# A feed-forward stage: a subtraction on another engine, a sum replaced by a read, and a block's products moved to the group's end

## Chip, cores and metric

The kernel runs on one core of a Trainium2 chip. The metric is the device time of one execution in microseconds, as the median of several runs. A core has TensorE (PE in the profile, with PEld for its weight loads), VectorE (DVE), ScalarE (ACT), GpSimd (POOL) and SyncE (SP). SP, ACT and POOL can each issue DMAs.

## The reference, cut to what matters

```python
# attention with a decay bias, 4 batches x 8 heads x 576 tokens x 64  ->  x [2304, 512]
h = x @ w_in                                   # w_in [512, 2048]
g = where(h >= 1, h, where(h <= -1, 0, (h + 1) ** 2 / 4))
x2 = g @ w_out                                 # w_out [2048, 512]
logits = x2 @ w_gate                           # [2304, 8]
# 8 experts with 288 tokens each, taken greedily by logit;
# out[mask] = relu(x2[mask] @ w1[e]) @ w2[e]
```

Each operand of the feed-forward products is split into a high part (`xh`, `ih`, `gh`, `oh`: a copy rounded to the matmul's float type) and a low part (`xl`, `il`, `gl`, `ol`: operand minus high part), and a product is the sum of three matmuls, high by high, high by low and low by high. The weights arrive as 64-bit numbers; the kernel converts them to 32-bit ones during the attention and keeps these in device memory, in the buffers `w32` (the flag `wide`).

## The kernel before, in words

Attention comes first, then the feed-forward, then routing and the experts. The change lies in the feed-forward (class `Ffn`).

The 2304 tokens go through in six groups of 384, numbered 0 to 5 here; each group goes through the 16 blocks of 128 columns of the hidden layer. The text calls a block's work `h(i)` (12 matmuls into the PSUM tile `ph`, of which there are three, L619) and `xmm(i)` (nine matmuls that add the block's part of x2 to the three PSUM tiles `px`, L656 to L658). Programs are written out in full, so every engine runs its own instructions in the order in which `run` issues them.

Between `h(i)` and `xmm(i)` stands a chain over three engines: VectorE clips `ph` to [-1, 1] (L627, "the clip"), ScalarE squares (L628), VectorE takes the maximum with `ph` (L639, "the maximum"), ScalarE copies the result into `gh` (L640), and GpSimd subtracts, `gl = u - gh` (L641). The finished pair waits in the list `pend` until two blocks are there; then the older one's `xmm` is issued. So `xmm(i)` comes after `h(i+2)` on TensorE, and blocks 14 and 15 of a group are added up after `h(0)` and `h(1)` of the next group. Then `tail` copies the three `px` tiles out (L665) and stores them.

At the end of each group but the last, the next group's x is split: right behind `h(15)` four ScalarE copies make `xh` (L605) and four VectorE subtractions `xl` (L606), since `h(15)` is the last to read the old ones.

VectorE also has a list of small jobs, `later`, taken up a few at a time: one by `some(1)` between the clip and the maximum, and three by `some(3)` at the block's end, from block 3 of group 1 on. These are the "dots": for each of the 8 experts a 128 x 512 multiplication with a gate row, summed along the row (L677). 120 of them make the logits of x2's rows (input `x`). 128 of them fold the gate into w_out (input `wt`, one 128 x 512 tile of w_out for 8 dots; two buffers). `fold` makes that tile on GpSimd as `oh + ol` (L706), each one issued with the first dot of the tile before it. The last group keeps its pairs (tiles `ghk`, `glk`), gets its logits by matmuls with the folded weights, and its products follow in `rest`.

In group 0 further work is on VectorE and GpSimd: the last steps of the attention (`norm`, `side_last`, called by `first(i)`) and the splits of the weights (`split_hi`, `split_lo`, L583 and L591).

Of the kernel before, what the change touches and what calls it, by code (L numbers as in the profile page):

```python
# [9 lines left out]
F32 = mybir.dt.float32  # L10
# [8 lines left out]
OP = mybir.AluOpType  # L19
# [5 lines left out]
def f(t):  # L25
    return t.bitcast(F32)
# [7 lines left out]
class Attention:  # L34
# [23 lines left out]
    def setup(self, identf):  # L58
        nc, c = self.nc, self.c
        S = self.S  # L60
        self.identf = identf
        st = self.w.tile([32, S], F32, name="s_in", tag="El")
        nc.scalar.dma_start(st, self.s.rearrange("b h s -> (b h) s"))
        self.load_first(0)
        zero = c.tile([128, 128], F32, name="zero")
# [63 lines left out]
        for h in range(2):  # L129
            nc.sync.dma_start(f(W)[64:66, h, :S], f(ck)[h:h + 1])  # L130
# [13 lines left out]
    def first_pair(self, h):  # L144

        X, Y, Z, W = self.stacks[0]
        for which in (1, 0):
            self.copy_hi(0, which, (h,))
        self.nc.gpsimd.tensor_scalar(Z[0:64, h], f(X)[0:64, h], 1.0, 0.0, op0=OP.mult, op1=OP.add)
        self.nc.vector.tensor_copy(Y[64:128, h, :self.S], f(Y)[0:64, h, :self.S])  # L150
        for which in range(2):
            self.prep_lo(0, which, (h,))
# [305 lines left out]
class Ffn:  # L458
# [3 lines left out]

    G = 384

    def __init__(self, tc, dr, raw, xp, t, xd, w_in, w_out, w_gate, x2d, L, wog, identf):
# [127 lines left out]
    def xload(self, g):  # L595
        self.xg = self.t.tile([128, 4, self.G], F32, name="xg", bufs=1)
        self.nc.sync.dma_start(self.xg, self.xd[:, g * self.G:(g + 1) * self.G].rearrange("(c p) t -> p c t", p=128))

    def xsplit(self):
        nc, G = self.nc, self.G  # L600
        self.x = []
        for c in range(4):
            xh = self.t.tile([128, G], F32R, name=f"xh{c}", bufs=1)
            xl = self.t.tile([128, G], F32R, name=f"xl{c}", bufs=1)
            nc.scalar.activation(xh, self.xg[:, c], AF.Copy)  # L605
            nc.vector.tensor_tensor(xl, self.xg[:, c], f(xh), op=OP.subtract)  # L606
            self.x.append((xh, xl))

    def h(self, i, keep, prep, x, x0):

        nc, G = self.nc, self.G
        ih, il = self.W["i", i]
        p = self.ps.tile([128, 512], F32, name="ph", tag="ph", bufs=3)
        n = 0
        for c in range(4):
            xh, xl = self.x[c]
            s = slice(c * 128, c * 128 + 128)
            for a, b in ((ih, xh), (ih, xl), (il, xh)):
                nc.tensor.matmul(p[:, :G], a[:, s], b, start=n == 0, stop=n == 11)  # L619
                n += 1  # L620
        if x:
            self.xsplit()
        if prep and i:
            self.split_hi("i", i + 2)

        u = self.t.tile([128, G], F32, name="u")
        nc.vector.tensor_scalar(u, p[:, :G], -1.0, 1.0, op0=OP.max, op1=OP.min)  # L627
        nc.scalar.activation(u, u, AF.Square, bias=self.half, scale=0.5)  # L628
        if prep and i:
            self.split_lo("i", i + 2)  # L630
        if not x0:
            self.some(1)
        if keep:
            gh = self.w[i // 8].tile([128, G], F32R, name="ghk", tag=f"ih{i}")
            gl = self.w[i // 8].tile([128, G], F32R, name="glk", tag=f"il{i}")
        else:
            gh = self.t.tile([128, G], F32R, name="gh", bufs=3)
            gl = self.t.tile([128, G], F32R, name="gl", bufs=3)
        nc.vector.tensor_tensor(u, p[:, :G], u, op=OP.max)  # L639
        nc.scalar.activation(gh, u, AF.Copy)  # L640
        (nc.vector if keep and i == self.NF - 1 else nc.gpsimd).tensor_tensor(gl, u, f(gh), op=OP.subtract)  # L641
        if prep:
            self.split_hi("o", i + 1)
            self.split_lo("o", i + 1)
            for j in {3: (), 4: ()}.get(i, (8, 9, 10) if i == 5 else (i + 5,)):
                self.load_in(j)
                self.load_out(j)
        return gh, gl
# [50 lines left out]

    def fold(self, i):  # L700

        oh, ol = self.W["o", i]

        def add():
            self.wt[i] = self.gp.tile([128, 512], F32, name="wt", bufs=2)
            self.nc.gpsimd.tensor_tensor(self.wt[i], f(oh), f(ol), op=OP.add)  # L706

        return add, self.dots(lambda: self.wt[i], self.wogf[:, i])

    def fold_split(self):  # L710
        nc, w, wf = self.nc, self.wog, self.wogf
# [56 lines left out]
    def run(self, ntok, first, second):  # L768

        nc, NF = self.nc, self.NF  # L770
        NG = ntok // self.G
        pend, later, ready = [], self.later, None
        for g in range(NG):
            end = g == NG - 1
            if end:
                self.fold_split()
            px, pl, own = [], None, []
            if not g:

                px += [self.ps.tile([128, 512], F32, name="px", tag="px", bufs=4) for _ in range(3)]  # L780
            for i in range(NF):
                if i == 2 and not end:
                    self.xload(g + 1)
                gp = self.h(i, end, g == 0, i == NF - 1 and not end, g == 1 and i < 3)
                if i == 2 and not end and g:
                    px += [self.ps.tile([128, 512], F32, name="px", tag="px", bufs=4) for _ in range(3)]
                if not g and i == 2:

                    p = self.ps.tile([128, 512], F32, name="busy", tag="px", bufs=4)
                    for _ in range(6):  # L790
                        nc.tensor.matmul(p[:, :self.G], self.W["i", 2][0][:, :128], self.x[0][0], start=True,
                                         stop=True)
                if len(pend) == 2 or (end and pend):
                    j, a, b, p, gg = pend.pop(0)
                    self.xmm(j, a, b, p, range(3))
                    if j == NF - 1:
                        ready = (gg, p)
                if end:
                    own.append(gp)
                    if i == 0:  # L800
                        pl = self.ps.tile([128, 512], F32, name="pl", tag="px", bufs=4)
                    if i >= 2:
                        self.logits(i - 2, *own[i - 2], pl)
                else:
                    pend.append((i,) + gp + (px, g))
                if ready:
                    gg, p = ready
                    ready = None
                    tails = [(3 * gg + t, self.tail(3 * gg + t, p[t])) for t in range(3)]
                    dots = [d for tt, x2 in tails for d in self.dots(lambda x2=x2: x2, self.L[:, tt])]  # L810
                    later[:0] = dots
                if g == 0:
                    first(i)
                if g > 1 - (i > 2) and (not end or i % 2 or i < 8):
                    self.some(1 if end else 3)
                if g == 0 and i == NF - 2:
                    second()
            if g == 0:

                adds, dots = zip(*[self.fold(i) for i in range(NF)])  # L820
                adds[0]()
                for i in range(NF):
                    nxt = adds[i + 1] if i + 1 < NF else lambda: None
                    later += [lambda a=nxt, d=dots[i][0]: (a(), d())] + dots[i][1:]
        self.some(len(later))
        self.own, self.ng, self.pl = own, NG, pl
# [23 lines left out]
class Route:  # L850
# [146 lines left out]
    def phase(self, k):  # L997
# [25 lines left out]
        run = t([128, 2 * J], BF16, "run")  # L1023
        ATf = AT.rearrange("p a j -> p (a j)")
        v.tensor_tensor_scan(run, ATf, self.iotf[:, 0:2 * J], 0.0, op0=OP.add, op1=OP.bypass)
        self.mark()
        ei = t([128, 1], I32, "ei", bufs=8)
# [189 lines left out]
class Experts:  # L1217
# [59 lines left out]
    def low(self, *args, **kw):  # L1277

        self.lows.append((self.a.t + 190, args, kw))
# [373 lines left out]
```

## Time and profile before

| | |
|---|---|
| median of 3 runs | 1049.25 us (1046.25 to 1054.68) |
| profiled execution | 1042.44 us, of which the span from first to last instruction is 1040.7 us |
| TensorE busy | 968.7 us, 93% of the span |
| VectorE busy | 790.0 us, 76% |
| ScalarE busy | 489.3 us, 47% |
| GpSimd busy | 455.1 us, 44% |
| mean granted TensorE clock | 0.980 of full speed |
| feed-forward groups 0 to 4 | 288.0 to 650.5 us of the span |

Matmuls overlap each other, so the duration of one (0.34 us for 384 columns) is about twice the distance to the next; the distance between starts is what counts. The same holds, less so, for VectorE: the next instruction starts a little before the one ahead of it has ended.

### The profile page before, as it was taken

What the parts mean: (1) busy time and instruction counts of PE and PEld (TensorE: products, weight loads), DVE (VectorE), ACT (ScalarE), POOL (GpSimd) and SP (SyncE); (2) the same over time, 40 slices, a digit from 0 to 9 for tenths busy, and PEclk for the clock granted to TensorE, in tenths of its full rate; (3) what the DMA queues carried; (4) which work ended last, traced back from release to release, by engine and by line L of the source; (5) the groups of instructions that cost most, each with busy time, mean ns of one, the idle gap of its engine ahead of it and who ended that gap; (6) DMA issues with size and microseconds to landing.
All of it is one profiled execution on the core that took longest, in us unless ns stands there. A gap on an engine that the chain in (4) does not pass through costs nothing.

```text
span 1040.7 us, 18588 instructions
## 1 busy us (share of the span) xinstructions
PE 968.7 (93%) x6479; PEld 856.2 (82%) x6479; DVE 790.0 (76%) x2029; ACT 489.3 (47%) x961; POOL 455.1 (44%) x471
## 2 busy tenths in 40 slices
PE   6899999999989999999899899999899979989996
PEld 5777777777768899888798798889788878879996
DVE  6688888988857667999999999885576687766510
ACT  5677777777745532322322322430245435536531
POOL 3245454445423233424424333330668868973211
PEclk9999999999999999999899899999899989999999
DMA  5767777878566040020020110101645455557400
GB/s 129 166 163 200 184 205 188 218 189 214 165 212 232 2 172 1 1 91 1 6 87 1 53 39 0 62 1 42 198 136 164 132 169 166 167 147 236 127 24 24
DMA packets 123067, 122.66 MB, mean 118 GB/s; under 512 B 73922, under 2 KB 90562, under 8 KB 122844
## 3 DMA queue, kind: packets, MB, share of 16 engines
q1 hardware_dynamic: 104604, 89.79, 30.8%
q0 software_dynamic: 17312, 30.55, 10.1%
q10 hardware_dynamic: 1056, 1.12, 0.4%
q8 instruction: 51, 0.84, 0.3%
q14 instruction: 44, 0.36, 0.1%
HBM read 89.36 MB, written 27.50 MB: 112 GB/s over the span
## 4 chain that ended last, share of the span: by engine, by line
PE 66%; DVE 22%; issue 5%; DMA 3%; ACT 2%; POOL 2%; SPq 0%; another core or an unknown queue 0%; POOLq 0%; DVEq 0%; ACTq 0%
PE ph L619 11%; PE py L1486 8%; PE ph L1434 8%; DVE junk L677 7%; PE po L333 6%; PE pst L301 6%; PE px L656 4%; PE px L658 4%; PE px L657 4%; PE ps L249 2%; DVE cmp L1212 2%; PE ps L250 2%; PE rp L1121 2%; PE pt L199 2%; DVE nm L259 2%
## 5 line engine op out<-in xcount | busy, mean ns | idle before, releaser
L641 POOL TENSOR_TENSOR gl<-u,gh 128x384 fp32r<-128x384 f32 x80 | 98.4, 1230 | 237.1 <-ACT gh L640 152.6
L1212 POOL TENSOR_TENSOR wl<-raw,wh 128x512 fp32r<-128x512 f32 x98 | 129.4, 1346 | 59.6 <-DMA raw<-in_moe_w_dram 33.8
L628 ACT ACTIVATE u<-u,half 128x384 f32<-128x384 f32 x96 | 59.2, 617 | 183.4 <-DVE u L627 180.9
L619 PE MATMUL ph<-xh,ih 128*128 128x384 f32 x384 | 132.2, 344 | 7.4 <-ACT xh L605 4.2
L619 PE MATMUL ph<-xl,ih 128*128 128x384 f32 x384 | 132.4, 345 | 4.1 <-DVE xl L606 4.1
L619 PE MATMUL ph<-xh,il 128*128 128x384 f32 x384 | 132.3, 345 | 3.0 <-DVE il L591 2.9
L677 DVE SCALAR_TENSOR_TENSOR junk<-wt,gb 128x512 f32<-128x512 f32 x128 | 116.7, 947 | 0.0
L333 PE MATMUL po<-E,V 128*128 128x320 f32 (+4 forms) x448 | 112.6, 379 | 0.4 <-ACT E L305 0.4
L677 DVE SCALAR_TENSOR_TENSOR junk<-x,gb 128x512 f32<-128x512 f32 x120 | 103.0, 888 | 4.5 <-ACT x L665 4.5
L656 PE MATMUL px<-oh,gh 128*128 128x512 f32 x240 | 96.0, 400 | 1.7 <-ACT x L665 1.7
L658 PE MATMUL px<-oh,gl 128*128 128x512 f32 x240 | 96.6, 402 | 0.7 <-POOL gl L641 0.7
L657 PE MATMUL px<-ol,gh 128*128 128x512 f32 x240 | 95.4, 398 | 0.0
L333 PEld LDWEIGHTS po<-E,V 128*128 128x128 f32 (+1 forms) x448 | 74.9, 191 | 20.1 <-issue 7.4
L619 PEld LDWEIGHTS ph<-xh,ih 128*128 128x128 f32 x384 | 73.5, 192 | 13.8 <-ACT xh L605 5.9
L1486 PE MATMUL py<-hh,wh 128*128 128x288 f32 x256 | 81.1, 317 | 0.0
L619 PEld LDWEIGHTS ph<-xl,ih 128*128 128x128 f32 x384 | 73.7, 192 | 8.7 <-DVE xl L606 5.2
L1212 ACT ACTIVATE wh<-raw 128x512 fp32r<-128x512 f32 x128 | 76.0, 623 | 9.2 <-DMA raw<-in_moe_w_dram 8.3
L1434 PE MATMUL ph<-xh,wh 128*128 128x288 f32 x256 | 79.1, 309 | 0.2 <-ACT xh L1212 0.2
L1434 PE MATMUL ph<-xl,wh 128*128 128x288 f32 x256 | 78.5, 307 | 0.5 <-DVE xl L1212 0.4
L1434 PE MATMUL ph<-xh,wl 128*128 128x288 f32 x256 | 78.1, 305 | 0.0
L619 PEld LDWEIGHTS ph<-xh,il 128*128 128x128 f32 x384 | 73.6, 192 | 4.8 <-DVE il L591 4.8
L1486 PE MATMUL py<-hl,wh 128*128 128x288 f32 x256 | 77.3, 302 | 0.0
(228 smaller groups left out, 2513.3 us busy)
## 6 DMA issues: line engine op xcount, KB each, us to landing
raw<-in_moe_w_dram SPq DMA_DIRECT2D x128, 256.0 KB
r<-in_moe_w_in_dram SPq DMA_DIRECT2D x16, 512.0 KB
r<-in_moe_w_out_dram SPq DMA_DIRECT2D x16, 512.0 KB
xg<-xd SPq DMA_DIRECT2D x6, 768.0 KB
x2d<-x SPq DMA_DIRECT2D x36, 128.0 KB
Y<-Y POOLq DMA_DIRECT2D x15, 288.0 KB
nk<-in_k_dram SPq DMA_DIRECT2D x32, 128.0 KB
nq<-in_q_dram SPq DMA_DIRECT2D x32, 128.0 KB
```

The source lines that it names most:

```text
L301: nc.tensor.matmul(pst[u][:, cols], l, r, start=first, stop=last, skip_group_check=u == "c" or u == "b")
L333: nc.tensor.matmul(t[:, 256 + c0:256 + g1], V[:b - a, kb, 64 * h:64 * h + 128], E[:b - a, e0:e0 + g1 - c0], start=i == 0, stop=i == len(or ...
L619: nc.tensor.matmul(p[:, :G], a[:, s], b, start=n == 0, stop=n == 11)
L628: nc.scalar.activation(u, u, AF.Square, bias=self.half, scale=0.5)
L641: (nc.vector if keep and i == self.NF - 1 else nc.gpsimd).tensor_tensor(gl, u, f(gh), op=OP.subtract)
L656: nc.tensor.matmul(px[t][:, cols], gh[:, s], oh[:, cols], start=i == 0, stop=False)
L657: nc.tensor.matmul(px[t][:, cols], gh[:, s], ol[:, cols], start=False, stop=False)
L658: nc.tensor.matmul(px[t][:, cols], gl[:, s], oh[:, cols], start=False, stop=last)
L677: self.nc.vector.scalar_tensor_tensor(junk, x(), 1.0, self.gb[:, e], op0=OP.mult, op1=OP.mult, accum_out=out[:, e:e + 1])
L1212: return fn(*a, **kw)
L1434: self.nc.tensor.matmul(p[:, :self.C], a[:, cols], b, start=c == 0 and i == 0, stop=c == 3 and i == 2)
L1486: nc.tensor.matmul(p[:, :C], a[:, o:o + 128], b[:, fb], start=fb == 0 and i == 0, stop=fb == 7 and i == 2)
```

## The change

1. `h` no longer issues `gl = u - gh` where it stood. It leaves it in `self.gl`, and `run` calls that at the block's end, behind `xmm`, the tails, `first(i)` and the dots. The engine is now VectorE. In the last group GpSimd still does it at the old place, except for block 15, which VectorE did before and still does, now at the block's end.
2. `fold` no longer adds `oh + ol` on GpSimd. It reads the tile from `w32` (here the inputs are 64-bit, so `wide` is true) by a DMA issued on the GpSimd queue, in the same place.
3. At block 15 of groups 0 to 4 both waiting pairs are taken from `pend`: `xmm(13)` and `xmm(14)` follow `h(15)`. The next group then starts with one pair waiting: `h(0)` is followed by `h(1)`, and `xmm(15)` comes behind `h(1)` as before. In the last group `xmm(15)` of group 4 comes behind `h(0)` and nothing behind `h(1)`.

```diff
         nc.scalar.activation(gh, u, AF.Copy)
-        (nc.vector if keep and i == self.NF - 1 else nc.gpsimd).tensor_tensor(gl, u, f(gh), op=OP.subtract)
+        low = lambda eng: eng.tensor_tensor(gl, u, f(gh), op=OP.subtract)
+        self.gl = lambda: low(nc.vector)
+        if keep and i < self.NF - 1:
+            self.gl = lambda: None
+            low(nc.gpsimd)
...
     def fold(self, i):
 
-        oh, ol = self.W["o", i]
-
-        def add():
+        def read():
             self.wt[i] = self.gp.tile([128, 512], F32, name="wt", bufs=2)
-            self.nc.gpsimd.tensor_tensor(self.wt[i], f(oh), f(ol), op=OP.add)
-
-        return add, self.dots(lambda: self.wt[i], self.wogf[:, i])
+            self.nc.gpsimd.dma_start(self.wt[i], self.w32[1][i] if self.wide else
+                                     self.w_out[i * 128:(i + 1) * 128])
+
+        return read, self.dots(lambda: self.wt[i], self.wogf[:, i])
...
-                if len(pend) == 2 or (end and pend):
+
+                for _ in range(min(1, len(pend)) if end else 1 + (i == NF - 1) if len(pend) == 2 else 0):
                     j, a, b, p, gg = pend.pop(0)
                     self.xmm(j, a, b, p, range(3))
...
                 if g > 1 - (i > 2) and (not end or i % 2 or i < 8):
                     self.some(1 if end else 3)
+
+                self.gl()
                 if g == 0 and i == NF - 2:
                     second()
             if g == 0:
 
-                adds, dots = zip(*[self.fold(i) for i in range(NF)])
-                adds[0]()
+                reads, dots = zip(*[self.fold(i) for i in range(NF)])
+                reads[0]()
                 for i in range(NF):
-                    nxt = adds[i + 1] if i + 1 < NF else lambda: None
+                    nxt = reads[i + 1] if i + 1 < NF else lambda: None
                     later += [lambda a=nxt, d=dots[i][0]: (a(), d())] + dots[i][1:]
```

## Rows read from the trace of the kernel before

**Rows 1.** Windows: length, busy (count) of PE PEld DVE ACT POOL, PEclk, DMA, GB/s.

```profile
363.10:430.96 67.86, 67.67 (x337) 61.03 (x338) 51.57 (x126) 22.60 (x42) 23.85 (x22) 1.00 0.19 67
430.96:503.29 72.33, 68.41 (x338) 60.31 (x336) 70.33 (x160) 20.22 (x37) 28.63 (x21) 1.00 0.10 33
503.29:578.04 74.75, 70.93 (x336) 62.98 (x336) 72.76 (x165) 21.40 (x40) 29.64 (x22) 0.95 0.10 33
578.04:650.45 72.41, 70.77 (x337) 63.19 (x337) 68.60 (x159) 21.41 (x40) 26.24 (x20) 0.95 0.10 33
650.45:662.20 11.75, 11.05 (x56) 9.85 (x56) 7.48 (x16) 6.08 (x12) 3.71 (x4) 1.00 0.03 11
```

**Rows 2.** Chain of waits in order of time: start, length, what (280 to 760 us).

```profile
410.08 2.11 PE ph L619 x12
...
471.02 1.50 DVE junk L677 x3
```

**Rows 3.** Timeline of VectorE in group 2: start, length, instruction.

```profile
472.92 1.31 DVE L677 SCALAR_TENSOR_TENSOR junk<-wt,gb 128x512 f32<-128x512 f32 x1
...
475.84 1.49 DVE L677 SCALAR_TENSOR_TENSOR junk<-wt,gb 128x512 f32<-128x512 f32 x1
...
477.26 0.55 DVE L627 TENSOR_SCALAR u<-ph 128x384 f32<-128x384 f32 x1
477.74 0.68 DVE L677 SCALAR_TENSOR_TENSOR junk<-wt,gb 128x512 f32<-128x512 f32 x1
...
478.50 0.56 DVE L639 TENSOR_TENSOR u<-ph,u 128x384 f32<-128x384 f32 x1
478.97 0.68 DVE L677 SCALAR_TENSOR_TENSOR junk<-wt,gb 128x512 f32<-128x512 f32 x1
...
480.19 1.49 DVE L677 SCALAR_TENSOR_TENSOR junk<-wt,gb 128x512 f32<-128x512 f32 x1
```

**Rows 4.** Timeline of GpSimd in the same stretch.

```profile
471.93 1.75 POOL L706 TENSOR_TENSOR wt<-oh,ol 128x512 f32<-128x512 f32 x1
475.45 1.33 POOL L641 TENSOR_TENSOR gl<-u,gh 128x384 fp32r<-128x384 f32 x1 [1.78 <-ACT gh L640]
```

**Rows 5.** Timeline of ScalarE in the same stretch.

```profile
479.15 0.53 ACT L640 ACTIVATE gh<-u 128x384 fp32r<-128x384 f32 x1 [0.68 <-PE px L657]
```

**Rows 6.** Timeline of TensorE at two group starts; in brackets the idle time before, and releaser.

```profile
444.04 0.50 PE L656 MATMUL px<-oh,gh 128*128 128x512 f32 x1 [1.70 <-ACT x L665]
...
503.29 0.44 PE L619 MATMUL ph<-xh,ih 128*128 128x384 f32 x1 [1.88 <-ACT xh L605]
...
505.36 0.69 PE L619 MATMUL ph<-xl,ih 128*128 128x384 f32 x1 [1.63 <-DVE xl L606]
...
509.05 0.63 PE L656 MATMUL px<-oh,gh 128*128 128x512 f32 x1
```

**Rows 7.** Line L606: count, min/median/max duration in ns.

```profile
L606 DVE TENSOR_TENSOR xl<-xg,xh x24: 545/547/1104, 281.1 to 652.4; 128x384 fp32r<-128x384 f32 x24
```

**Rows 8.** Timeline of VectorE and TensorE in group 0's first blocks.

```profile
300.87 1.09 DVE L591 TENSOR_TENSOR ol<-ol,oh 128x512 fp32r<-128x512 f32 x1 [1.11 <-ACT oh L583]
...
301.55 0.42 PE L658 MATMUL px<-oh,gl 128*128 128x512 f32 x1
...
303.55 0.50 DVE L627 TENSOR_SCALAR u<-ph 128x384 f32<-128x384 f32 x1
...
304.70 0.44 PE L619 MATMUL ph<-xh,il 128*128 128x384 f32 x1 [0.99 <-DVE il L591]
```

**Rows 9.** Timeline of GpSimd, VectorE and ScalarE around DMAs issued on GpSimd's queue.

```profile
283.88 0.85 POOL L375 DMA_DIRECT2D R<-rd  x1
...
284.26 0.68 DVE L502 SCALAR_TENSOR_TENSOR ce<-r,ce 128x512 int32<-128x512 int32 x1
...
290.67 0.57 POOL L523 DMA_DIRECT2D w32i<-co  x1 [0.30 <-POOL co L505]
...
295.58 0.63 ACT L583 ACTIVATE ih<-il 128x512 fp32r<-128x512 f32 x1 [5.47 <-DMA il<-w32i]
```

## The prediction

> **What bounds the kernel now.** I read the busy times by stretch first, cut at the first matmul of each of groups 1 to 5 (the last stretch is group 5's first three blocks), because the page's averages mix stages with different limits. Groups 1 to 4 hold the same matmuls, yet take 67.86, 72.33, 74.75 and 72.41 us [rows 1]. Group 1 is TensorE's own pace: TensorE is busy in 67.67 of its 67.86 us, VectorE in 51.57. Without the two short stalls at its start (0.6 us together) a block is (67.86 - 0.6) / 16 = 4.20 us, half of it `h`, half `xmm`. In groups 2 to 4 VectorE is busy 95 to 97% of the time, and TensorE has gaps. The chain of waits says the same: in group 1 it runs over `ph`, one block after the other, later over the dots [rows 2].
>
> The timeline of VectorE shows why. A dot takes 0.68 us and the next instruction starts 0.61 us after it, but some take 1.3 to 1.5 us: the ones that start at 475.84 and at 472.92 [rows 3]. Beside the first, GpSimd runs `gl` (475.45 to 476.78), beside the second the sum for `wt` (471.93 to 473.68) [rows 4]. The long dot ends about one dot's length after the GpSimd instruction does: it waits that out. So every block loses 0.8 us to `gl`, and every second block another 0.5 to 0.6 us to `wt`. From long dot to long dot a block takes 480.19 - 475.84 = 4.35 us, the one with `wt` 475.84 - 471.02 = 4.82 [rows 2, 3]: 4.58 on average, above TensorE's 4.20. The Trainium skill has this as a rule (SBUF — State Buffer, section Who interferes with whom): a VectorE instruction with two inputs in SBUF and a GpSimd instruction that reads SBUF lock each other out for a whole instruction. By that rule the trace agrees, with 1.49 us for 0.68.
>
> VectorE's lag is paid at the group's end. `xl` comes late, TensorE stands for 1.88 and 1.63 us at 503.29 and 505.36 [rows 6], and then runs slowly: a matmul with 512 columns takes 0.63 us at 509.05, even the one at 444.04, just after a wait, 0.50; the granted clock of groups 3 and 4 is 0.95 against 1.00 [rows 1, 6].
>
> **The change, part by part.**
>
> *The low part on VectorE.* GpSimd loses 80 subtractions, VectorE gains them. The nearest row for one is `xl`, of the same shape with two SBUF inputs: 0.547 us [rows 7], or 0.47 until the next can start, as behind the maximum (478.50 to 478.97 [rows 3]). I take 0.47, upper end 0.55. It waits for `gh`, which ends at 479.15 + 0.53 = 479.68 [rows 5], 1.2 us after the maximum began; the three dots behind the maximum last until 478.97 + 3 x 0.61 = 480.8, so they hide the wait. Where no dots are left (groups 0 and the start of 1) VectorE waits some 0.7 us there, in blocks where it has over 1 us to spare. Behind the waiting instruction stands the next clip, and behind that all of the next block.
>
> *VectorE's block afterwards*, dots undisturbed: clip to maximum with one dot and the square between, 478.50 - 477.26 = 1.24; maximum to first dot 0.47; three dots 3 x 0.61 = 1.83 (478.97 to 480.19 is two of them); `gl` 0.47 [rows 3]. Sum 4.01 us (4.09 at the upper end), against TensorE's 4.20. Over a group: 16 x 4.01 = 64.2, four `xl` 4 x 0.55 = 2.2, and one wait for the first dot on a row of x2, which needs the tails (the same copies hold TensorE for 1.70 us at 444.04 [rows 6]; I take 1.2). That is 67.6, at the upper end 68.9 plus 0.5; TensorE needs 16 x 4.20 = 67.2, and I allow 0.6 for waiting on the tails' copies, 67.8. It is nearly a draw, with TensorE's side winning by little. I take 67.8 per group, upper end 69.4.
>
> *Lag and products.* `gl(i)` is needed by the third matmul of `xmm(i)`, 8.4 + 0.47 us after `h(i)` ends. At a group's start VectorE does `xl` and the rest of a block first, about 2 + 4 us, so `gl` is in time with over 2 us to spare. With both products behind `h(15)`, TensorE has 4.2 us of work where it had 2.1 before it needs `xh` and `xl`; ScalarE and VectorE need about 0.7 + 2.2 us for those once VectorE has no lag. So the stalls and the slow clock behind them go. The work is only moved: the next group has one `xmm` less between `h(0)` and `h(1)`.
>
> *The read instead of the sum.* 16 sums go; 16 DMAs of 256 KB come. GpSimd's issue of a DMA takes 0.57 to 0.85 us, and the two-input instruction of VectorE that ran beside one at 284.26 took its ordinary 0.68 us [rows 9], so I take no cost on VectorE. A tile is read when the dots of the tile before the last are over, and has 8 dots, two blocks or 8.4 us, to land; what queues behind it on GpSimd is the next read and, in group 5, `glk`, when all reads are done. Landing: a write of 256 KB issued at 290.67 and the read of the same tile behind it were both over at 295.58, 4.9 us for two transfers [rows 9]. The bounds are 2.5 and 4.9 us; either is hidden by the dots. The Trainium skill (DMA: Bandwidth & Descriptors, section Anatomy of one DMA) gives 2.0 us and the bytes at 436 GB/s, an estimate of 2.6 us; no run here shows a lone one.
>
> *Group 0.* Here `gl(i)` falls behind `norm` and `side_last`. In block 0 it comes just ahead of the clip that begins at 303.55; what `gl` adds to VectorE (0.47) it saves on `ol`, which took 1.09 us beside GpSimd's `gl` instead of 0.69 [rows 8]. But the matmul that needs `gl(0)` ran at 301.55 and now waits till about 303.7: 2.1 us. Of that, TensorE's 0.99 us stall at 304.70 is absorbed. Net loss 1.1 us (0 to 3, since blocks 1 to 3 repeat it more weakly). Later in group 0 the exchange is even.
>
> *Group 5.* GpSimd keeps its subtraction, so its pace stays. Its first three blocks took 11.75 us [rows 1] where TensorE's work is 3 x 2.1 + 2 x 2.1 = 10.5.
>
> **The sum.** Group 2: 72.33 - 67.8 = 4.5. Group 3: 74.75 - 67.8 = 6.9. Group 4: 72.41 - 67.8 = 4.6. Start of group 5: 1.2. Stalls at the start of group 1: 0.6. Group 0: -1.1. Together 16.7 us; with the upper ends (three groups at 69.4, group 0 at -3) 10.0, with no loss in group 0 and no wait on the tails 19.6. The routing and the experts follow from the last group's logits and should shift as they are. On the profiled execution (span 1040.7 us and 1.7 around it, which stays) this is 1042.4 - 16.7 = 1025.7 us. The median of the runs lies 6.8 us above that execution, so I forecast 1032.5 us.
>
> **Rivals.**
>
> *VectorE stays the bound.* The issue of a read might lock out a dot as GpSimd's sums did. A group has 5 reads; each may cost up to 0.85 us [rows 9]. Then VectorE needs 67.6 + 4.2 = 71.8 us, 4.0 more than the 67.8 taken, in three groups: gain 16.7 - 12 = 4.7, up to 10 with the milder subtraction cost; time about 1042. Against it speaks the row at 284.26, for it that this is a single row. By the Trainium skill (SBUF — State Buffer, section Who interferes with whom) an instruction that only writes SBUF does not lock out a two-input one, which would exclude this.
>
> *Slower: the reads come late.* If a read takes L from release to landing and L exceeds 8.4 us, VectorE stands, with `gl` and the next clip behind it. Four reads of a group stand without rows of x2 to bridge them, 13 in all. The gain is used up at L = 8.4 + 16.7 / 13 = 9.7 us; at 12 us the loss is 13 x 3.6 - 16.7 = 30 us, time 1079. The 4.9 us for two transfers speaks against it, at a DMA load far above that of groups 2 to 4 (share 0.10 [rows 1]). The Trainium skill warns of such reads (SBUF — State Buffer, section SBUF: two separate sides): a DMA issued by GpSimd starves while VectorE runs a copy-like instruction from SBUF to SBUF in its double-port mode. By that rule nothing happens here, since the clip reads PSUM and the others have two inputs.
>
> *The gain is not carried to the end.* The time won until group 5 is waited for later, in group 5 or the routing: about 1049. Speaking for it: group 5 is bound by VectorE and GpSimd, untouched. Against it: its blocks start from the same chain, only earlier.
>
> **Chances.** Forecast 0.72; VectorE stays the bound 0.14; not carried 0.07; slower 0.07. A measurement of this kernel can tell about 1% from no change (the three runs lie 0.8% apart), which is 10.5 us. The forecast's lower end and a part of the second rival count as faster: 0.70 + 0.05 = 0.75. Within 1%: 0.18. Slower: 0.07. The range runs from 1049.25 - 19.6, less 5 us for the runs' scatter, to the second rival's 1042 and 2 us more: 1025 to 1044.
>
> **What the next profile would show.** Groups 1 to 4 at 67 to 69.5 us each, TensorE's clock 1.00 throughout them; dots of 0.68 us only, and a VectorE block of 4.0 us; no idle time ahead of the first `ph` matmuls of a group; in group 0 a wait of `px` on `gl`. I am wrong if dots stay above 1 us, if VectorE waits on `wt` from DMA, or if groups 1 to 4 shrink and the span doesn't.

## The result, and the profile after

The changed kernel takes 1032.84 us (median of 4 runs, 1032.08 to 1040.74) against 1049.76 us before (median of 4, 1046.25 to 1054.68): a ratio of 0.9854, 95% interval 0.9816 to 0.9892. The forecast was 1032.5 us, range 1025 to 1044.

First the busy time by stretch of the changed kernel, to lay beside [rows 1]: groups 0 to 4, then group 5's `h(0)`, `xmm(15)`, `h(1)` and `h(2)`. The columns are window and length in us, busy us (and count) of PE, PEld, DVE, ACT and POOL, granted clock, DMA share, GB/s.

```profile
292.11:370.88 78.77, 71.24 (x339) 62.42 (x339) 49.93 (x91) 38.30 (x70) 5.50 (x8) 0.96 0.46 146
370.88:438.14 67.26, 67.26 (x337) 60.89 (x336) 53.44 (x145) 22.68 (x41) 1.69 (x5) 1.00 0.22 75
438.14:505.80 67.66, 67.55 (x337) 60.82 (x336) 63.79 (x178) 20.67 (x39) 2.73 (x5) 1.00 0.18 55
505.80:574.36 68.56, 67.55 (x337) 60.82 (x336) 65.21 (x182) 21.67 (x40) 2.73 (x5) 1.00 0.18 54
574.36:642.65 68.29, 67.55 (x337) 60.82 (x336) 62.34 (x172) 22.18 (x41) 1.64 (x3) 1.00 0.15 47
642.65:651.10 8.45, 8.45 (x47) 7.96 (x46) 4.91 (x14) 3.22 (x6) 1.01 (x1) 1.00 0.26 87
```

Groups 1 and 2 now run at TensorE's pace: it is busy in all but 0.1 us of them. In groups 3 and 4 it still stands for 1.0 and 0.7 us. Its clock stays at 1.00 in all four. GpSimd, 24 to 30 us busy per group before, has 2 to 3. VectorE's timeline in the stretch of [rows 3] (start, length, instruction) has lost its long dots:

```profile
473.81 0.55 DVE L642 TENSOR_TENSOR gl<-u,gh 128x384 fp32r<-128x384 f32 x1
474.28 0.55 DVE L628 TENSOR_SCALAR u<-ph 128x384 f32<-128x384 f32 x1
474.75 0.68 DVE L682 SCALAR_TENSOR_TENSOR junk<-wt,gb 128x512 f32<-128x512 f32 x1
...
475.57 0.56 DVE L640 TENSOR_TENSOR u<-ph,u 128x384 f32<-128x384 f32 x1
476.05 0.68 DVE L682 SCALAR_TENSOR_TENSOR junk<-wt,gb 128x512 f32<-128x512 f32 x1
...
477.88 0.56 DVE L642 TENSOR_TENSOR gl<-u,gh 128x384 fp32r<-128x384 f32 x1
478.35 0.55 DVE L628 TENSOR_SCALAR u<-ph 128x384 f32<-128x384 f32 x1
```

From clip to clip it is 478.35 - 474.28 = 4.07 us, with no idle time shown, below TensorE's 4.20. The lines of the tiles `wt` and `junk` (min/median/max in ns) say it of all 128 folding dots, and give the price of issuing a read. Of the 120 dots on rows of x2, 11 still take over 1 us; all of them start after 647 us, in group 5, where GpSimd goes on subtracting.

```profile
L682 DVE SCALAR_TENSOR_TENSOR junk<-wt,gb x128: 680/684/691, 419.1 to 633.9; 128x512 f32<-128x512 f32 x128
...
L709 POOL DMA_DIRECT2D wt<-w32o x16: 546/546/562, 323.9 to 618.6; - x16
...
L682 DVE SCALAR_TENSOR_TENSOR junk<-x,gb x120: 674/684/1408, 384.2 to 682.0; 128x512 f32<-128x512 f32 x120
```

What TensorE still waits for, by its timeline (idle time and releaser in brackets): the low part in group 0's first blocks, and the copies of the previous group's rows in groups 3 and 4.

```profile
308.20 0.50 PE L663 MATMUL px<-oh,gl 128*128 128x512 f32 x1 [0.96 <-DVE gl L642]
...
318.10 0.50 PE L663 MATMUL px<-oh,gl 128*128 128x512 f32 x1 [0.80 <-DVE gl L642]
...
323.98 0.50 PE L663 MATMUL px<-oh,gl 128*128 128x512 f32 x1 [1.43 <-DVE gl L642]
...
516.10 0.50 PE L661 MATMUL px<-oh,gh 128*128 128x512 f32 x1 [1.01 <-ACT x L670]
```

The two profiled executions differ by less than the medians: spans of 1040.7 and 1031.1 us, 9.6 us. In three pieces: the stage starts at 292.11 instead of 288.03 us (+4.1); from there to the end of group 5's third `h`, a point where both orders have done the same work, it takes 359.0 instead of 374.0 us (-15.0); the rest takes 380.0 instead of 378.7 us (+1.3). The 4.1 us lie in the attention, which the change does not touch; the chain of waits of the changed kernel has there

```profile
201.46 10.99 DMA nq<-in_q_dram
```

a load of q that came late in this execution. Over the thirteen kernels profiled for this study, all with the same attention, the stage starts between 286.1 and 293.1 us. So **the stretch of 374.0 and 359.0 us is the measure below**; the scatter of single runs, about 1% (1046.25 to 1054.68 us before), hides what is smaller than some 8 us.

### The profile page after: what moved, and what is told of

It reads as the page before. It is cut to its first block, busy times and chain, and to the rows that moved or that the text cites. A ratio compares the mean times of both kernels' runs of the same rounds, so it can differ in the third digit from the quotient of the medians.

```text
span 1031.1 us, 18509 instructions
## 1 busy us (share of the span) xinstructions
PE 964.3 (94%) x6479; PEld 854.7 (83%) x6479; DVE 768.1 (74%) x2109; ACT 490.2 (48%) x961; POOL 338.8 (33%) x391
## 4 chain that ended last, share of the span: by engine, by line
PE 58%; DVE 24%; DMA 5%; issue 5%; ACT 5%; POOL 1%; SPq 1%; another core or an unknown queue 0%; POOLq 0%; ACTq 0%; DVEq 0%
PE py L1493 8%; PE ph L1441 8%; PE ph L620 8%; PE po L333 6%; PE pst L301 6%; DVE junk L682 6%; PE px L661 3%; PE px L663 3%; PE px L662 3%; ACT u L629 3%; PE ps L249 2%; PE ps L250 2%; DVE u L628 2%; DVE gl L642 2%; PE rp L1128 2%
## 5 line engine op out<-in xcount | busy, mean ns | idle before, releaser
L682 DVE SCALAR_TENSOR_TENSOR junk<-x,gb 128x512 f32<-128x512 f32 x120 | 84.9, 737 | 4.5 <-ACT x L670 4.5
L682 DVE SCALAR_TENSOR_TENSOR junk<-wt,gb 128x512 f32<-128x512 f32 x128 | 82.9, 685 | 0.0
L1493 PE MATMUL py<-hh,wl 128*128 128x288 f32 x256 | 77.2, 302 | 0.0
L506 POOL TENSOR_TENSOR co<-cm,ce 128x512 f32<-128x512 f32 x32 | 40.5, 1264 | 104.2 <-ACT cm L505 99.4
```

The source lines that it names most:

```text
L506: nc.gpsimd.tensor_tensor(out, f(m), f(e), op=OP.mult)
L682: self.nc.vector.scalar_tensor_tensor(junk, x(), 1.0, self.gb[:, e], op0=OP.mult, op1=OP.mult, accum_out=out[:, e:e + 1])
L1493: nc.tensor.matmul(p[:, :C], a[:, o:o + 128], b[:, fb], start=fb == 0 and i == 0, stop=fb == 7 and i == 2)
```

## The experiments

One table for all. The stretch goes from the first `ph` matmul of group 0 to the end of `h(2)` of group 5 (its first matmul's start plus 2.11 us for the twelve; the 374.2 us in the first expectation runs to the last matmul's end); groups are from first `ph` matmul to first `ph` matmul. Ratios are to the kernel before, on the same chip as the row's kernel, with 95% intervals.

| kernel | stretch, us | groups 1, 2, 3, 4, us | ratio |
|---|---|---|---|
| before | 374.0 | 67.9, 72.3, 74.8, 72.4 | 1 |
| changed | 359.0 | 67.3, 67.7, 68.6, 68.3 | 0.9854 (0.9816 to 0.9892) |
| e1: low part alone | 372.4 | 67.9, 71.8, 73.7, 71.4 | 1.0021 (0.9983 to 1.0059) |
| e2: read alone | 367.7 | 67.9, 69.6, 72.4, 72.0 | 0.9880 (0.9836 to 0.9925) |
| e3: products alone | 373.5 | 67.3, 74.2, 74.4, 71.3 | 0.9978 (0.9938 to 1.0018) |
| e4: low part and read | 358.9 | 67.9, 67.3, 68.5, 68.3 | 0.9804 (0.9765 to 0.9844) |
| e5: GpSimd fills | 353.1 | 67.3, 67.3, 67.3, 67.3 | 0.9771 (0.9712 to 0.9829) |
| e6: one buffer | 407.4 | 68.4, 85.4, 85.0, 81.8 | 1.0330 (1.0254 to 1.0407) |
| e7: group 0 on GpSimd | 356.9 | 67.3, 67.6, 68.6, 68.3 | 0.9852 (0.9785 to 0.9918) |
| e8: low part ahead of the dots | 388.9 | 67.3, 79.8, 79.2, 78.6 | 1.0148 (1.0085 to 1.0211) |
| e9: e7 and dots later | 355.3 | 67.3, 67.7, 67.7, 67.7 | 0.9789 (0.9750 to 0.9829) |
| e10: changed, again | 358.5 | 67.3, 67.6, 68.6, 68.3 | 0.9883 (0.9836 to 0.9930) |
| e11: e7, again | 356.9 | 67.3, 67.7, 68.6, 68.3 | 0.9835 (0.9797 to 0.9873) |

**e1, the low part alone.** Of the three edits only the first:

```diff
-        (nc.vector if keep and i == self.NF - 1 else nc.gpsimd).tensor_tensor(gl, u, f(gh), op=OP.subtract)
+        low = lambda eng: eng.tensor_tensor(gl, u, f(gh), op=OP.subtract)
+        self.gl = lambda: low(nc.vector)
...
+                self.gl()
```

> The low part moves to VectorE behind the dots; the sum for the folding stays on GpSimd and each group still ends with one product. Measured over the stretch from the first ph matmul of group 0 to the end of the third block's h in group 5: 374.2 us in the kernel before, 359.0 in the changed one. Theory (VectorE and GpSimd lock each other out of two-input instructions, and VectorE's lag is what costs): dots go back to 0.68 us except one in 16, those beside the sum, which stay at about 1.3; VectorE's block is 4.08 us, 4.7 with the sum, so groups 2 to 4 take some 69.6 us each; the stretch is 363 to 365 us, the kernel about 1.0% faster than before. Rival (it is the second product at the group's end, which hides the splitting of x, that brought the gain): stalls ahead of the first ph matmul of groups 3 and 4 stay near 3 us with the slow clock behind them; the stretch is 370 us or more.

Measured: 1.6 us won in the stretch, not 9 to 11, and no gain in the runs. My expectation fell, by one sum: I let GpSimd's sum cost a dot 0.6 us. In its timelines, GpSimd first, then VectorE, it hits the low part instead, and costs it 1.1 us:

```profile
473.20 1.61 POOL L710 TENSOR_TENSOR wt<-oh,ol 128x512 f32<-128x512 f32 x1 [33.29 <-DVE junk L681]
```

```profile
473.59 1.65 DVE L641 TENSOR_TENSOR gl<-u,gh 128x384 fp32r<-128x384 f32 x1
...
478.75 0.55 DVE L641 TENSOR_TENSOR gl<-u,gh 128x384 fp32r<-128x384 f32 x1
```

With the low part gone from GpSimd, the sum runs as soon as the last dot of the old tile frees its buffer, and the low part, one dot further on, waits for its end: 1.65 us instead of 0.55. Two folding blocks then take 2 x 4.08 + 1.1 = 9.3 us against 9.17 before; what e1 wins comes mostly from the blocks whose dots are on rows of x2, 4.08 us each instead of 4.35. The stalls stay, as the rival had it, though shorter: 0.91 us ahead of the first `ph` matmul of groups 3 and 4 and 1.30 behind it, 2.2 together where it was 3.5. The rival's reason, the missing second product, is tested in e3.

**e2, the read alone.** Only `fold` reads instead of adding.

> Only the sum on GpSimd is replaced by the read. Theory of the lock: of the long dots those beside the sum vanish (0.68 us), those beside the low part stay at 1.5; VectorE's block is 4.35 us throughout, still above TensorE's 4.20; groups 2 to 4 lose about 2.3 us each, the stretch is 366 to 369 us, the kernel 0.5 to 0.8% faster. Rival (the reads come late or lock VectorE out): VectorE waits for wt from the DMA, or dots beside a read are longer than 0.7 us; no gain or a loss. Rival of the products: nothing changes at the group starts, 374 us.

Measured: 6.3 us won, in line with the first theory, if unevenly: groups 2 to 4 gave 2.8, 2.3 and 0.4 us instead of 2.3 each. The tile's lines also have what the trace before could not show, the landing of a read; on VectorE the dot beside the low part stays long.

```profile
L677 DVE SCALAR_TENSOR_TENSOR junk<-wt,gb x128: 673/684/1504, 419.4 to 645.7; 128x512 f32<-128x512 f32 x128
...
DMA to landing us min/median/max: 2.8/2.9/3.7
```

```profile
475.32 1.50 DVE L677 SCALAR_TENSOR_TENSOR junk<-wt,gb 128x512 f32<-128x512 f32 x1
```

**e3, the products alone; e4, the other two without them.** One line put in or taken out:

```diff
-                if len(pend) == 2 or (end and pend):
+                for _ in range(min(1, len(pend)) if end else 1 + (i == NF - 1) if len(pend) == 2 else 0):
```

> Only the products: blocks 13 and 14 behind the last h of a group. Theory of the lag: VectorE stays the bound with 4.58 us per block, the stalls only move from the group's start into its blocks, and what can be won is the slow clock behind the 3.5 us stalls, which costs nothing while VectorE is the bound: stretch 371 to 375 us, the kernel the same within 0.3%. Rival (the products bring the gain): the stalls of 3.5 us and the slow clock at groups 3 and 4 and 1 us at group 5 go for good, 8 to 13 us, stretch 361 to 366 us.

> The changed kernel with one product at the group's end as before. Theory of the lag: VectorE is ahead of its due time at the group's end, so xh and xl come while the one product runs; stalls at group starts under 0.5 us, stretch 359 to 361 us, within 0.2% of the changed kernel. Rival of the products: each group start stalls by 1.5 us or more, the clock falls again, stretch 365 us or more.

Measured: 0.5 us won by the products alone, nothing lost without them. In e3 the stall of group 3's start has only moved into the products, as TensorE's timeline shows:

```profile
503.18 0.50 PE L656 MATMUL px<-oh,gh 128*128 128x512 f32 x1 [1.45 <-ACT gh L640]
...
504.63 0.55 PE L658 MATMUL px<-oh,gl 128*128 128x512 f32 x1 [0.73 <-POOL gl L641]
```

In e4 one product of 2.1 us covers the splitting of x as well as two do, except at the start of group 1 (a stall of 0.59 us), and group 2 is 0.35 us shorter there. Over the whole stretch the products are worth nothing.

**e5, a GpSimd instruction that reads nothing.** The kernel before, with zeros instead of the low part in groups 0 to 4 (the low part of `h` is missing from the output):

```diff
+            nc.gpsimd.memset(f(gl), 0.0)
```

> The kernel before, but in groups 0 to 4 GpSimd fills gl with zeros instead of subtracting (the low part of h is left out of the output there); the sum for the folding and the order stay. GpSimd still has an instruction in the same place with the same waits, but one that reads nothing. Theory (two-input instructions of VectorE and GpSimd instructions that read lock each other out): dots beside the fill take 0.68 us, only those beside the sum 1.3; VectorE's block is 3.6 us, 4.2 with the sum, so TensorE sets the pace; stretch from group 0's first ph matmul to the end of group 5's third h 357 to 360 us (before 374.0, changed 359.0). Rival (any GpSimd instruction at work, or the crossing of engines by itself, makes the dot long): the dot beside the fill is longer by the fill's length, stretch 366 to 374 us.

Measured: 20.9 us won, more than the 14 to 17 expected, 1.8 of it in group 0; TensorE sets the pace in groups 1 to 4. One thing differs from what I wrote: the fill does not wait for `gh`, only for its buffer, and so runs earlier in the block. It still runs beside dots. Nor can the gain be that the products no longer wait for the low part: in groups 1 to 4 of the kernel before, that wait came to 0.7 us in all. The timelines of GpSimd and of VectorE:

```profile
478.65 0.42 POOL L644 MEMSET gl<- 128x384 f32 x1 [1.19 <-PE px L661]
```

```profile
478.52 0.68 DVE L680 SCALAR_TENSOR_TENSOR junk<-wt,gb 128x512 f32<-128x512 f32 x1
479.13 0.69 DVE L680 SCALAR_TENSOR_TENSOR junk<-wt,gb 128x512 f32<-128x512 f32 x1
```

Neither waits for the other. The sum still reads, and of the 128 folding dots three take 1.3 us, each beside a sum; no other takes over 0.71. The Trainium skill's rule for an instruction that only writes SBUF (SBUF — State Buffer, section Who interferes with whom) agrees with this trace, 0.68 us beside a fill of 0.42.

**e6, reads without cover.** The changed kernel with `bufs=1` for `wt`, and each read issued with its own first dot:

```diff
-                reads[0]()
                 for i in range(NF):
-                    nxt = reads[i + 1] if i + 1 < NF else lambda: None
-                    later += [lambda a=nxt, d=dots[i][0]: (a(), d())] + dots[i][1:]
+                    later += [lambda a=reads[i], d=dots[i][0]: (a(), d())] + dots[i][1:]
```

> The changed kernel with one buffer for wt instead of two, each read issued just ahead of its own first dot, so that nothing covers it. It prices the reads that come late. Theory (a read costs nothing only because eight dots cover it): VectorE stands about 3.5 us (2.9 us from issue to landing, the issue and two semaphores) ahead of the first dot of each of 16 tiles, and with it the low part and the next clip; less VectorE's room of 0.1 us per block, some 3.2 us a tile: stretch 359 + 45 = 400 to 410 us, the kernel about 3% slower than before. Rival (VectorE's queue is not what sets the pace, the products have two blocks of room): stretch under 370 us.

Measured: 48.4 us lost, 3.0 for each of 16 tiles, and 3.3% slower than before. VectorE's timeline and the tile's list of waits (releaser: us, times):

```profile
489.81 0.69 DVE L682 SCALAR_TENSOR_TENSOR junk<-wt,gb 128x512 f32<-128x512 f32 x1 [3.27 <-DMA wt<-w32o]
```

```profile
  DMA wt<-w32o: 49.4, 15
```

This is the slower rival, made to happen: 49.4 / 15 = 3.3 us per tile, which in the changed kernel lies under eight dots.

**e7 and e11, the low part of group 0 left to GpSimd.**

```diff
-        if keep and i < self.NF - 1:
+        if prep or (keep and i < self.NF - 1):
```

> The changed kernel, with the low part left to GpSimd at its old place in group 0 alone. Theory (in group 0 the low part stands in VectorE's queue behind the last steps of the attention, and the first four blocks' products wait for it): the waits of px on gl in group 0 go, 1.5 us are won there, stretch 357 to 358 us, the rest as in the changed kernel. Rival (those waits only take the place of waits for il, which come back): 358.5 to 359.5 us.

> The changed kernel with GpSimd's low part in group 0, once more: stretch 356.9 us within 0.3, about 0.2% faster than the changed kernel, which the runs' scatter may hide.

Measured: 356.9 us both times (expected: 357 to 358, then 356.9), 2.1 and 1.6 less than the changed kernel (359.0 and 358.5). The waits on the low part go (3.4 us over four blocks), and two waits on `il` come back (0.57 and 1.15 us): both theories held in part.

**e8, the low part right behind the maximum.** On VectorE as in the changed kernel, but at the old place in `h`.

> The changed kernel, with VectorE's low part issued right behind the maximum, ahead of the dots. Theory (the dots hide the wait for gh): VectorE stands 0.7 to 0.8 us ahead of each low part, its block is 4.8 us instead of 4.08, groups 2 to 4 take 78 to 81 us each, stretch 390 to 398 us, the kernel 1.5 to 2.5% slower than before. Rival (the place does not matter, an earlier low part even helps the products): stretch 358 to 362 us.

Measured: 29.9 us lost, 1.1 less than the least I expected, and 1.5% slower than before. VectorE's timeline:

```profile
489.49 0.56 DVE L640 TENSOR_TENSOR u<-ph,u 128x384 f32<-128x384 f32 x1 [0.41 <-ACT u L629]
490.70 0.56 DVE L642 TENSOR_TENSOR gl<-u,gh 128x384 fp32r<-128x384 f32 x1 [0.65 <-ACT gh L641]
```

VectorE stands some 0.65 us in every block for `gh` (31.2 us over the 48 blocks of groups 2 to 4), with the next clip queued behind. That the low part stands behind the dots is as needed as that it left GpSimd.

**e9, the rows' dots one block later.** On top of e7; beside it the changed kernel again (e10).

```diff
-                    later[:0] = dots
+                    later[3:3] = dots
```

> The changed kernel with the low part of group 0 on GpSimd, and the dots on the rows of x2 put behind the next three jobs of the list instead of at its head, so that VectorE folds the gate for one more block while ScalarE copies the rows out. Theory (what is left above TensorE's pace in groups 2 to 4 is VectorE's wait of 1.1 us for the first row, its lag, and TensorE's wait of 0.7 to 1.0 us on those copies): the waits go, groups 2 to 4 take 67.3 to 67.6 us each, stretch 354 to 355.5 us (with group 0 alone mended 356.9, changed 359.0). Rival (the wait on the copies is ScalarE's own and stays): stretch 356.5 to 357 us.

> The changed kernel once more, on the same chip as the two versions beside it: stretch 359.0 us within 0.3, 1.3 to 1.7% faster than before.

Measured: 355.3 us, groups 2 to 4 even, and no wait of TensorE on the copies left. The busy times of its groups 2 to 4:

```profile
433.71:501.38 67.67, 67.55 (x337) 60.82 (x336) 64.75 (x181) 21.43 (x40) 2.68 (x5) 1.00 0.17 55
501.38:569.05 67.67, 67.56 (x338) 60.82 (x336) 65.32 (x181) 22.12 (x40) 2.68 (x5) 1.00 0.18 55
569.05:636.71 67.66, 67.55 (x337) 60.82 (x336) 61.86 (x170) 22.02 (x40) 1.61 (x3) 1.00 0.15 47
```

On the same chip it took 1025.72 us against e10's 1033.84 (medians of 6 each), and the two intervals in the table do not touch. Of these 8 us the stretch explains 358.5 - 355.3 = 3.2; the other 5 lie in stages that e9 leaves alone, and are scatter as far as these runs show. By its median e9 is the fastest version that computes the reference, ahead of both kernels; its interval overlaps that of e11. The repeat e10 came out a little off what I wrote for it: 358.5 us instead of 359.0 within 0.3, and 1.2% faster than before instead of 1.3 to 1.7.

## Why the prediction was right, point by point

**What bounds the kernel.** Right. Long dots were the lockout, and the lag it built up was the loss: e5, in which GpSimd fills where it subtracted, brings groups 1 to 4 to 67.3 us each.

**VectorE's block.** Right in kind, wrong on who wins the draw. The block was forecast at 4.01 us and takes 4.07: the maximum waits for ScalarE's square, so that clip to maximum is 475.57 - 474.28 = 1.29 us instead of the 1.24 that I took. Over a group this makes 16 x 4.07 = 65.1; the block with the four `xl` takes 1.9 us more (forecast 2.2), the one with the first row of x2 1.2 more (forecast 1.2). Together 68.2 us, where I had 67.6 for VectorE and 67.8 for TensorE. TensorE alone needs 67.3 (e5). So in groups 3 and 4, which take 68.6 and 68.3 us, it is still VectorE that sets the pace, by about 1 us. Its list of waits over the whole of group 3 (us, times, longest) has no wait for `ph`, only the one for the first row:

```profile
DVE junk L682 <- ACT x L670: 1.1, 1, 1.1
```

TensorE's 1.01 us at 516.10, which I had as a term of its own, is the same lag seen from the other side. On ScalarE's timeline the copies of the rows stand behind `gh`, and `gh` waits for VectorE's maximum:

```profile
515.04 0.52 ACT L641 ACTIVATE gh<-u 128x384 fp32r<-128x384 f32 x1 [0.69 <-DVE u L640]
515.47 1.56 ACT L670 ACTIVATE x<-px 128x512 f32<-128x512 f32 x3
```

In e9, where VectorE folds on instead of waiting for the row, both waits are gone and the three groups take 67.7 us. The 67.8 us per group that I took became 67.7, 68.6 and 68.3.

**The read.** Right on each count: the 128 dots take at most 0.691 us, though 14 of the 16 issues run beside one, so issuing locks nothing out; a read lands in 2.9 us (e2, median; 2.8 to 3.7), between the bounds of 2.5 and 4.9; and two blocks of dots hide it (e6: 3.3 us per tile where they don't). The Trainium skill's 2.0 us and the bytes at 436 GB/s (DMA: Bandwidth & Descriptors, section Anatomy of one DMA), an estimate of 2.6 us, are a little below the measured 2.9.

**Lag and products.** Half wrong, with little effect on the sum. I put down the end of the stalls at the group starts to the second product's cover as well as to the vanished lag. e3 and e4 leave the products only the 0.6 us at the start of group 1, won in e3 and lost in e4, which has most of it back in group 2; the rest is the lag's.

**Group 0.** Forecast -1.1 us. It took 78.77 us with `xmm(14)` now inside; without those 2.1 us that is 76.67 against 363.10 - 288.03 = 75.07: -1.6. The same kernel in e10 comes to -1.1; most of the difference is TensorE's wait for `ih` at 300.69, 3.60 us against 3.21 in e10, which lies ahead of the first `gl`. The net came near the forecast, its parts did not. Waits on `gl` came in four blocks, 3.4 us (4.0 in e10), where I had counted on the first almost alone; and waits on `il` went in three blocks, 0.99 + 0.58 + 1.16 = 2.7 us, of which I had counted 0.99.

**Group 5 and the sum.** Cut where the stretch ends, the start of group 5 took 11.58 us before (the 11.75 of [rows 1] runs to the last matmul's end) and takes 8.45 + 2.1 = 10.55, with the product moved out of it; forecast 10.5. Term by term the stretch gives 4.7 + 6.2 + 4.1 + 1.0 + 0.6 - 1.6 = 15.0 where 16.7 was forecast. The shortfall lies in groups 3 and 4 (1.2), where VectorE still holds TensorE up, and in group 0 (0.5).

**The rest of the span, and the median.** Behind the stretch it took 378.7 us before and 380.0 after. But the changed kernel again, in e10, took 386.9, and the kernels profiled lie between 378.7 and 387.6, so one profile of each shows only to within some 8 us that the gain was carried through. The granted clock of this piece was 0.97 in the two profiles compared and 0.95 in the four longest; whether the clock or the length comes first is not shown. The medians say more: 16.9 us won in the result and some 13 in e10, on either side of the stretch's 15. I had added 6.8 us for the median's place above the profiled execution; the changed kernel's profiled execution lies at its median, and the two profiled spans differ by 9.6 us, not 16.7. That the forecast came within 0.3 us of the median is luck. What was right is the stretch, 15.0 of 16.7 us, and why.

**What the prediction did not see** is that the first two edits need each other. Alone they win 1.6 and 6.3 us, together 15.1 (e4). Two folding blocks took VectorE 9.17 us before; with the low part moved alone they take 9.3, with the read alone 2 x 4.35 = 8.7, and only with both 2 x 4.07 = 8.14, less than TensorE's 8.4.

## What to carry to other kernels

In these traces a VectorE instruction with two inputs in SBUF that met one of GpSimd's subtractions or sums waited for its end, so work that seems free on GpSimd cost the other engine much of its length (0.6 to 1.1 us per dot or low part): look for two lengths of one instruction in a timeline and lay GpSimd's beside it. When two engines are near a draw, sum each one's work per block, since edits that win little alone may cross the line together, and add what comes once a group: it decided the draw here. Put an instruction that waits for another engine behind work that is ready, and price a hidden transfer by taking its cover away.

## What was not expected

The attention's length moves from execution to execution: the same attention ends, and the feed-forward starts, anywhere from 286.1 to 293.1 us, in the changed kernel's profile by 10.99 us in the chain on one load of q. A stretch cut at the same instructions repeats far better: 359.0 and 358.5 us, 356.9 and 356.9. And a fill by GpSimd beside a two-input instruction costs neither anything (0.42 and 0.68 us), while a subtraction of the same size costs a dot 0.8 us.
